# Nine more units of the first token group take seven products in layer two; Sinkhorn's matmuls stand later and in one bank

## The chip, the cores and the metric

The kernel runs on one core of one Trainium2 chip. The metric is device time in microseconds (us): 2010.24 us, the median of three runs (2008.88 to 2013.74). Engines are named as the profile names them: PE is TensorE (PEld its weight loads), DVE VectorE, ACT ScalarE, POOL GpSimd, SP the engine that issues DMAs.

## The reference

Three stages follow each other: windowed attention (4 batches, 8 heads, 576 positions), a two-layer network with a leaky ReLU, and a mixture of eight experts whose token weights come from eight rounds of Sinkhorn scaling. The last stage takes three quarters of the time:

```python
logits = x @ w_gate                       # x: 2304 x 512, 8 experts
P = np.exp(logits - logits.max())
for _ in range(8):
    P /= P.sum(1, keepdims=True) + 1e-09
    P /= P.sum(0, keepdims=True) + 1e-09
    P *= N / E
for e in range(E):
    h = np.maximum(x @ w1[e], 0.0)        # 512 -> 1024
    ye = h @ w2[e]                        # 1024 -> 512
    out += P[:, e:e + 1] * ye
```

## The kernel before

Every fp32 operand is split in two parts, a rounded high part and the rest (the low part), and `three` (L362 to L364) makes three matmuls of one: high by high, high by low, low by high. A split costs one copy on ACT (L1142 for weights) and one subtraction (L585) on DVE or POOL, whichever the planner picks.

The expert stage (function `second`) works through 48 units: three token groups of 768 tokens (`sb_`, 0 to 2), each with 16 half experts (`g`, 0 to 15; a half expert is 512 of the 1024 hidden columns). Unit u is `sb_ = u // 16`, `g = u % 16`. The text calls the token groups the first (units 0 to 15), the second (16 to 31) and the third (32 to 47). In a unit, layer one multiplies two matrices cut in 2x2 blocks by a Strassen-like scheme with seven block products in place of eight (`PRODUCTS`): 84 matmuls of 384 columns into the PSUM tiles W01 and X01. Layer two then works on three token strips, with either the same seven products (three strips of seven products of six matmuls, 126 matmuls of 256 columns; `layer2`) or the plain eight (144 matmuls; `direct`). `plain2(u)` says which; before the change units 2 to 15 are plain and all others take seven.

The two forms load the other engines differently. Seven products need sums of weight blocks (S1 to S4 for layer one, T1 to T4 for layer two) and sums of hidden blocks; each output block is gathered by DVE from six products of 256 columns per strip (L1466). The plain form needs the weights only as they are, and gathers two outputs of 512 columns per strip (L1393). `weights(m, u)` prepares the weights of layer m + 1: it loads the raw block, and then either makes seven operands of it with all their sums ("full": seven ACT copies and eleven block operations on DVE or POOL) and writes what later groups need to DRAM (`wfar`), or makes plain operands alone (four or three copies and as many subtractions), or fetches finished operands from `wfar`. Before the change layer one's weights are made in full in the first group, and layer two's in the second group, because the first group needs them plain. The weights of the first two half experts are made ahead for both layers (`convert_ahead`, eight jobs) during the two-layer network, on ACT and POOL.

Each engine runs its own queue in order. The order is written by a planner: `add` collects operations with an engine (or a choice), a cost, a priority (mostly a due time) and the keys that they read and write; `arrange` walks through simulated time and always starts the ready operation with the lowest priority number. The cost marker "2" tells it that a DVE operation and POOL keep each other out. A PSUM bank, such as SW[1], is a key: whoever writes it waits for the last reader.

Sinkhorn (`sinkhorn`, L1058 to L1097) is a chain: in a round, eight small DVE instructions and one PE matmul (L1087) that sums over partitions into bank SW[1]. Its DVE steps have priority 33, its PE steps -50. Bank SW[1] is also used by layer two of the first units.

Of the kernel before, what the change touches and what calls it, by code (L numbers as in the profile page):

```python
# [13 lines left out]
ALU = mybir.AluOpType  # L14
# [5 lines left out]
DM = H * D  # L20
F1 = 2048
E, F2 = 8, 1024
# [18 lines left out]
HA = SB // 2  # L41
NSB = NT // SB
NG = 2 * E
PRE = 2


def key_start(j):
# [11 lines left out]
def program(tc, qk, v, moe_w_in, moe_w_out, moe_alpha, moe2_w_gate, moe2_w1, moe2_w2, masks, out):  # L59
# [697 lines left out]
    class Op:  # L757


        def __init__(self, engines, emit, prio, deps, slots, seq):  # L760
            self.engines, self.emit, self.prio, self.slots, self.seq = dict(engines), emit, prio, slots, seq
            self.lock = {"POOL"} | ({"DVE"} if len(engines) > 1 and engines[0][0] == "DVE" or "2" in dict(engines) else set())
            self.engines.pop("2", None)
            self.deps, self.next, self.wait, self.ready = deps, [], 0, 0.0

    queue_of, ops = {}, []
    writer, readers = {}, {}
# [27 lines left out]
    def arrange(places, more):  # L795
# [46 lines left out]
        while len(done) < len(ops):  # L842
            best = None
            for e, l in lists.items():
                if l:
                    t = max(now[e], min(at(o, e) for o in l))
                    if best is None or t < best[0]:
                        best = t, e
            assert best is not None, ("stuck", [(b.name, b.left) for c in queue_of for b in queue_of[c][heads[c] : heads[c] + 2]], heads, len(done))
            t, e = best  # L850
            o = min((o for o in lists[e] if at(o, e) <= t), key=lambda o: (o.prio, o.seq))
            cost = o.engines[e]
            for e2 in o.engines:
                lists[e2].remove(o)
            if e in o.lock and e in held:
                held["POOL" if e == "DVE" else "DVE"] = t + cost
            if e == "SP":
                begin = max(t + 1.2, wire[0])
                wire[0] = begin + cost
                end, now[e] = wire[0] + 0.8, t + 0.06  # L860
            else:
                end = now[e] = t + cost
            o.at, o.on, o.end = t, e, end
            done.append(o)
            for c, ats in more.get(o, {}).items():
                free[c] += [(end, at) for at in ats]
                bind(c)
            late = end + (0.25 if e == "PE" else 0.1)
            for x in o.next:
                x.ready = max(x.ready, end if e in x.engines and e != "SP" and len(x.engines) == 1 else late)  # L870
                x.wait -= 1
                if x.wait == 0:
                    enlist(x)
            for b in o.slots:
                b.left -= 1
                b.end = max(b.end, late)
                if b.left == 0:
                    free[b.cls].append((b.end, b.at))
                    bind(b.cls)
        return sorted(done, key=lambda o: o.at)  # L880

    def second():
# [3 lines left out]
        step1, step2 = 29.5 / 7, 29.5 / 21  # L886

        def plain2(u):
            return u < NG and u >= PRE

        begins = [T1ST]
        for u in range(NSB * NG + 2):
# [165 lines left out]
        def sinkhorn():  # L1058
            G = ("SW", 1)
            g = SW[1]  # L1060
            R = "right"
            M = mem

            def v(cost, emit, reads, writes):
                add([("DVE", cost)], emit, 33, [*reads, R], writes)

            V = nc.vector
            v(0.35, lambda _: V.tensor_reduce(M["m1"], lgt.rearrange("p t e -> p (t e)"), axis=AX.X, op=ALU.max), ["lgt"], ["m1"])
            add([("PE", 0.1)], lambda _: nc.tensor.transpose(g[:1, :P], M["m1"], ident), -50, ["m1"], [G])
            v(0.3, lambda _: V.tensor_reduce(M["m2"], g[:1, :P], axis=AX.X, op=ALU.max), [G], ["m2"])  # L1070
            add([("PE", 0.1)], lambda _: nc.tensor.matmul(g[:, 0:1], ones[0:1, :], M["m2"], start=True, stop=True), -50, ["m2"], [G])
            v(0.15, lambda _: V.tensor_scalar(out=M["ng"], in0=g[:, 0:1], scalar1=-1.0, scalar2=None, op0=ALU.mult), [G], ["ng"])
            add([("ACT", 0.4)], lambda _: nc.scalar.activation(M["pt"], lgt, AF.Exp, bias=M["ng"], scale=1.0), -50, ["ng", "lgt"], ["pt"])
            for _ in range(8):
                v(0.29, lambda _: V.tensor_reduce(M["rr"], M["pt"], axis=AX.X, op=ALU.add), ["pt"], ["rr"])
                v(0.38, lambda _: V.tensor_scalar(out=M["rr"], in0=M["rr"], scalar1=EPS, scalar2=None, op0=ALU.add), ["rr"], ["rr"])
                v(0.27, lambda _: V.reciprocal(M["rr"], M["rr"]), ["rr"], ["rr"])
                v(
                    0.31,
                    lambda _: V.tensor_tensor(  # L1080
                        out=M["pt"], in0=M["pt"], in1=M["rr"].unsqueeze(2).to_broadcast([P, NTT, E]), op=ALU.mult
                    ),
                    ["rr", "pt"],
                    ["pt"],
                )
                v(0.44, lambda _: V.tensor_reduce(M["cs"], M["pt"].rearrange("p t e -> p e t"), axis=AX.X, op=ALU.add), ["pt"], ["cs"])
                add([("PE", 0.1)], lambda _: nc.tensor.matmul(g[:, :E], share, M["cs"], start=True, stop=True), -50, ["cs"], [G])  # L1087
                v(0.16, lambda _: V.tensor_scalar(out=M["rc"], in0=g[:, :E], scalar1=EPS * E / NT, scalar2=None, op0=ALU.add), [G], ["rc"])
                v(0.2, lambda _: V.reciprocal(M["rc"], M["rc"]), ["rc"], ["rc"])
                v(  # L1090
                    0.54,
                    lambda _: V.tensor_tensor(
                        out=M["pt"], in0=M["pt"], in1=M["rc"].unsqueeze(1).to_broadcast([P, NTT, E]), op=ALU.mult
                    ),
                    ["rc", "pt"],
                    ["pt"],
                )  # L1097

        def weights(m, u):
# [5 lines left out]
            nd = {n: need(m, u, i) for i, n in enumerate(names)}  # L1105
            cls = ("w1", "w2")[m]
            b = got[m, u] = {}
            full = g >= PRE and sb_ == m
            plain, sums = PLAIN[m], {s[0]: s[1:] for s in SUMS[m]}
            ready = [] if full or eight else [n for n in names if (g, m, n) in wfar]  # L1110
            if full:
# [244 lines left out]
        def direct(u, j, s, t0, tts):  # L1356
# [4 lines left out]
            e = g // 2  # L1361
            scaled = sb_ > 0 or e > 0
            for i, (a, x, r, d) in enumerate(EIGHT):
                ps, K = ((SW[s], ("SW", s)), (SX[s], ("SX", s)))[r - 1]
                t = t0 + 2 * i * step2

                def mm(_, i=i, a=a, x=x, ps=ps, d=d):
# [19 lines left out]

                def out_(_, ps=ps, oi=oi, tt=tt):
                    o, p_ = mem["o"][:, oi], mem["pt"][:, tt, e : e + 1]
                    if not scaled:  # L1390
                        nc.vector.tensor_tensor(out=o, in0=ps, in1=o, op=ALU.add)
                    else:
                        nc.vector.scalar_tensor_tensor(out=o, in0=ps, scalar=p_, in1=o, op0=ALU.mult, op1=ALU.add)  # L1393

                assert g
                add([("DVE", 0.75)], out_, t + 0.7, [K, "right", *okeys] + (["pt"] if scaled else []), okeys)
                if g == NG - 1:
                    send(oi, tt, t)

# [9 lines left out]
        def layer2(u):  # L1409
            sb_, g = divmod(u, NG)  # L1410
            h, w = got["h", u], got[1, u]
            e = g // 2
            scaled = sb_ > 0 or e > 0
            eight = plain2(u)
            for j in range(3):
                k = 3 * u + j
# [7 lines left out]
                for i, (a, x, bk) in enumerate(PRODUCTS):  # L1424
# [30 lines left out]
                    def out_(e_, ps=ps, oi=oi, dh=dh, tt=tt, new=new):  # L1455
                        o = mem["o"][:, oi, dh * FS : (dh + 1) * FS]
                        x = ps[:, :FS]
                        p_ = mem["pt"][:, tt, e : e + 1]
                        if new and not scaled:
                            nc.scalar.copy(o, x)  # L1460
                        elif new:
                            nc.scalar.mul(o, x, p_)
                        elif not scaled:
                            nc.vector.tensor_tensor(out=o, in0=x, in1=o, op=ALU.add)
                        else:
                            nc.vector.scalar_tensor_tensor(out=o, in0=x, scalar=p_, in1=o, op0=ALU.mult, op1=ALU.add)  # L1466

                    rd = [K, "right"] + ([] if new else [ok]) + (["pt"] if scaled else [])
                    add(act(FS, True) if new else dve(FS), out_, t, rd, [ok])
                    if sb_ == 0 and g == 1 and i in (5, 6):  # L1470

                        def scale(_, oi=oi, tt=tt):
                            o = mem["o"][:, oi]
                            nc.scalar.mul(o, o, mem["pt"][:, tt, 0:1])

                        add(act(DM), scale, t, ["pt", ("o", oi, 0), ("o", oi, 1)], [("o", oi, 0), ("o", oi, 1)])
                    if g == NG - 1 and i in (5, 6):
                        send(oi, tt, t)

# [46 lines left out]
    with tc.manual_schedule():  # L1526
# [33 lines left out]
                ahead = 30 if THIRD[0] <= n < THIRD[1] else 6  # L1560
                ready.setdefault(i, []).append((n, which, 12, begin[due] - ahead))
        n_ends = next(i for i, u in enumerate(units) if u[3] == order[-2])
        jobs = [(g, m, st) for g in range(PRE) for m in range(2) for st in range(2)]

        prev = None
        for i, u in enumerate(units[:-1]):
            if i == n_close:
# [5 lines left out]
                prep[0] = pool(sx, "prep", bufs=2, side="right")  # L1573
                pz = pool(sp, "pz", bufs=2, space=PSUM)
                banks += [(pz, "x"), (pz, "y")]
                last = len(units) - 4
                for x, job in enumerate(jobs):
                    pside.add(convert_ahead(*job), 19, begin[i + 3 + (last - i - 3) * (x + 1) // len(jobs)])
            if i >= 2 and units[i - 2][5]:
# [106 lines left out]
```

## Time and profile before

| | us |
|---|---|
| median of three runs | 2010.24 |
| lowest, highest | 2008.88, 2013.74 |
| the profiled execution | 2013.85 |
| its span, first to last instruction | 2012.1 |

The span is the time between the first and the last instruction that the profiler saw; 1.75 us of the profiled execution lie outside it. A matmul's busy time overlaps the next one's, so that PE's pace is read from how many matmuls stand in a stretch in which PE never waits. A unit's first layer-one matmul was taken as its start; units 8 and 14 start at 779.41 and 969.34 us, units 22 and 31 at 1219.24 and 1485.01 us, unit 0 at 522.0 us.

### The profile page before, as it was taken

How to read it: one execution, taken by the hardware profiler on the slowest of the kernel's cores; microseconds unless marked ns; L12 is line 12 of the kernel's file. 1: busy time of each engine (PE TensorE's matmuls, PEld its weight loads, DVE VectorE, ACT ScalarE, POOL GpSimd, SP SyncE). 2: the span in 40 equal slices, each digit the busy share in tenths (PEclk: the TensorE clock that was granted, in tenths of full speed). 3: DMA queues.
4: the chain of work that ended last, by engine and by line, in shares of the span. 5: the costliest groups of instructions: out<-in, count | busy, mean ns of one | idle time of the engine just before them, and what ended most of it. 6: DMA issues, size and time to landing. Idle time of an engine off the chain costs nothing.

```text
span 2012.1 us, 37421 instructions
## 1 busy us (share of the span) xinstructions
PE 1965.2 (98%) x14899; PEld 1940.5 (96%) x14899; DVE 1328.8 (66%) x2142; ACT 894.8 (44%) x1686; POOL 654.6 (33%) x567
## 2 busy tenths in 40 slices
PE   7999999999989999999999999999999999999998
PEld 5889999999979999999999999999999999999998
DVE  6775776764587645454536888778776666766766
ACT  6654444434445434343324545445444434434442
POOL 4434776676343232232200443233330001101100
PEclk8999999999999999999999999999999999999999
DMA  7421333332646845455486786677689667666662
GB/s 234 141 70 53 106 118 98 100 116 81 257 159 256 290 160 207 169 187 195 171 330 222 285 292 230 215 244 244 218 291 343 227 212 233 230 208 224 237 212 84
DMA packets 124014, 399.95 MB, mean 199 GB/s; under 512 B 12736, under 2 KB 41152, under 8 KB 118464
## 3 DMA queue, kind: packets, MB, share of 16 engines
q1 hardware_dynamic: 123840, 397.56, 57.4%
q8 instruction: 117, 1.92, 0.4%
q14 instruction: 57, 0.47, 0.1%
HBM read 283.22 MB, written 114.29 MB: 198 GB/s over the span
## 4 chain that ended last, share of the span: by engine, by line
PE 92%; DVE 4%; POOL 1%; DMA 1%; issue 1%; ACT 1%; SPq 0%; POOLq 0%; DVEq 0%; ACTq 0%
PE SW L364 7%; PE SW L362 7%; PE SW L363 7%; PE W L362 6%; PE W L363 6%; PE W L364 6%; PE SX L364 5%; PE SX L363 5%; PE SX L362 5%; PE X L363 5%; PE X L362 5%; PE X L364 5%; PE psH L362 3%; PE psH L364 3%; PE psH L363 3%; PE psY L362 3%
## 5 line engine op out<-in xcount | busy, mean ns | idle before, releaser
L362 PE MATMUL W<-XS,WT 128*128 128x384 f32 x768 | 260.3, 339 | 1.7 <-DVE WX L1340 1.2
L363 PE MATMUL W<-XS,WT 128*128 128x384 f32 x768 | 259.5, 338 | 0.0
L364 PE MATMUL W<-XS,WT 128*128 128x384 f32 x768 | 259.4, 338 | 0.0
L585 POOL TENSOR_TENSOR WT<-rawR,WT 128x512 fp32r<-128x512 f32 x78 | 104.8, 1345 | 377.4 <-ACT WT L1142 236.2
L362 PE MATMUL X<-XS,WT 128*128 128x384 f32 x576 | 194.4, 338 | 0.0
L1466 DVE SCALAR_TENSOR_TENSOR oR<-SW,pt,oR 128x256 f32<-128x256 f32 x282 | 132.8, 480 | 93.1 <-PE SW L364 91.7
L363 PE MATMUL X<-XS,WT 128*128 128x384 f32 x576 | 193.8, 336 | 0.0
L364 PE MATMUL X<-XS,WT 128*128 128x384 f32 x576 | 193.8, 336 | 0.0
L1466 DVE SCALAR_TENSOR_TENSOR oR<-SX,pt,oR 128x256 f32<-128x256 f32 x270 | 128.0, 479 | 71.6 <-PE SX L364 71.6
L391 POOL TENSOR_TENSOR gl<-u,gh 128x288 fp32r<-128x288 f32 x126 | 107.4, 854 | 154.3 <-ACT gh L390 147.7
L585 POOL TENSOR_TENSOR wR<-rawR,wR 128x512 fp32r<-128x512 f32 x36 | 51.2, 1425 | 314.0 <-ACT wR L1142 233.6
L363 PE MATMUL psH<-XS,WT 128*128 128x288 f32 x504 | 149.7, 297 | 1.3 <-DVE XS L142 1.3
L362 PE MATMUL psH<-XS,WT 128*128 128x288 f32 x504 | 150.7, 299 | 0.1
L364 PE MATMUL psH<-XS,WT 128*128 128x288 f32 x504 | 149.8, 297 | 0.0
L362 PEld LDWEIGHTS W<-XS,WT 128*128 128x128 f32 x768 | 145.6, 190 | 2.2 <-DVE WX L1340 1.4
L363 PEld LDWEIGHTS W<-XS,WT 128*128 128x128 f32 x768 | 145.1, 189 | 0.0
L364 PEld LDWEIGHTS W<-XS,WT 128*128 128x128 f32 x768 | 145.1, 189 | 0.0
L585 POOL TENSOR_TENSOR wR<-RAW,wR 128x512 fp32r<-128x512 f32 x38 | 54.3, 1432 | 252.1 <-ACT wR L1142 124.5
L387 DVE SCALAR_TENSOR_TENSOR u<-neg,rest,psH 128x288 f32<-128x288 f32 x108 | 55.3, 512 | 109.0 <-ACT neg L386 103.6
L363 PE MATMUL psY<-gl,WT 128*128 128x288 f32 x376 | 111.5, 297 | 5.1 <-POOL gl L391 5.0
L362 PE MATMUL psY<-gh,WT 128*128 128x288 f32 x376 | 113.1, 301 | 1.0 <-ACT acc L410 1.0
L364 PE MATMUL psY<-gh,WT 128*128 128x288 f32 x376 | 111.2, 296 | 1.4 <-POOL WT L532 1.4
(268 smaller groups left out, 6577.9 us busy)
## 6 DMA issues: line engine op xcount, KB each, us to landing
RAW<-in_moe_w SPq DMA_DIRECT2D x21, 1024.0 KB, 6.9
rawR<-in_moe_w SPq DMA_DIRECT2D x21, 1024.0 KB, 6.1
WT<-a11g SPq DMA_DIRECT2D x34, 512.0 KB, 4.9
WT<-S2g SPq DMA_DIRECT2D x34, 512.0 KB, 4.5
WT<-a12g SPq DMA_DIRECT2D x34, 512.0 KB, 3.6
WT<-S3g SPq DMA_DIRECT2D x34, 512.0 KB, 3.6
WT<-S1g SPq DMA_DIRECT2D x34, 512.0 KB, 3.7
WT<-a22g SPq DMA_DIRECT2D x34, 512.0 KB, 4.7
```

What stands on the lines that cost most here:

```text
L362: nc.tensor.matmul(ps, lh, rh, start=start, stop=False, skip_group_check=more)
L363: nc.tensor.matmul(ps, lh, rl, start=False, stop=False, skip_group_check=more)
L364: nc.tensor.matmul(ps, ll, rh, start=False, stop=stop, skip_group_check=more)
L387: nc.vector.scalar_tensor_tensor(out=u, in0=neg, scalar=rest[:, ft : ft + 1], in1=ps[:, :CH], op0=ALU.mult, op1=ALU.add)
L391: nc.gpsimd.tensor_tensor(out=gl, in0=u, in1=f(gh), op=ALU.subtract)
L585: eng.tensor_tensor(out=out, in0=x, in1=y, op=op)
L1466: nc.vector.scalar_tensor_tensor(out=o, in0=x, scalar=p_, in1=o, op0=ALU.mult, op1=ALU.add)
```

## The change

`plain2` now follows a list: units 0, 1, 2, 5, 8, 11 and 14 are plain, and the other nine of the first group (3, 4, 6, 7, 9, 10, 12, 13, 15) take seven products. Units 0 and 1, which took seven, become plain. So 7 units are plain in place of 14. `weights` follows: for the nine units both layers' weights are made in full in the first group, and the second group fetches layer two's sums; for the seven plain ones layer two's are still made in full in the second group. Only half expert 0's layer one is made ahead (two jobs in place of eight), and those jobs are due earlier.

Sinkhorn's DVE steps get priority 45 (33 before), its PE steps 45 (-50 before), and a PE step is planned no sooner than 1.5 us after the DVE step that writes its operand (`slack`). Three of its DVE steps per round are marked as keeping POOL out. The plain units 0 and 1 use the banks SW[0], SX[0] and SX[1] in turn, so that only Sinkhorn writes SW[1] until unit 2's layer two. Unit 0's outputs are copied by ACT, unit 1's are added by DVE and then scaled by ACT.

```diff
-PRE = 2
+PRE = 1
+EIGHTH = (0, 1, 2, 5, 8, 11, 14)
...
-                x.ready = max(x.ready, end if e in x.engines and e != "SP" and len(x.engines) == 1 else late)
+                x.ready = max(x.ready, end if e in x.engines and e != "SP" and len(x.engines) == 1 else late + x.slack)
...
         def plain2(u):
-            return u < NG and u >= PRE
+            return u < NG and u in EIGHTH
...
-            def v(cost, emit, reads, writes):
-                add([("DVE", cost)], emit, 33, [*reads, R], writes)
+            def v(cost, emit, reads, writes, both=False):
+                add([("DVE", cost), ("2", 0)][: 1 + both], emit, 45, [*reads, R], writes)
+
+            def pe(emit, reads):
+                add([("PE", 0.1)], emit, 45, reads, [G])
+                ops[-1].slack = 1.5
...
-                add([("PE", 0.1)], lambda _: nc.tensor.matmul(g[:, :E], share, M["cs"], start=True, stop=True), -50, ["cs"], [G])
+                pe(lambda _: nc.tensor.matmul(g[:, :E], share, M["cs"], start=True, stop=True), ["cs"])
...
-            full = g >= PRE and sb_ == m
+            full = (m == 1 or g >= PRE) and sb_ == (m if plain2(g) else 0)
...
-                ps, K = ((SW[s], ("SW", s)), (SX[s], ("SX", s)))[r - 1]
+                ps, K = ((SW[s], ("SW", s)), (SX[s], ("SX", s)))[r - 1] if g > 1 else (
+                    (SW[0], ("SW", 0)),
+                    (SX[0], ("SX", 0)),
+                    (SX[1], ("SX", 1)),
+                )[(2 * j + r - 1) % 3]
...
-                    if not scaled:
+                    if g == 0:
+                        nc.scalar.copy(o, ps)
+                    elif not scaled:
                         nc.vector.tensor_tensor(out=o, in0=ps, in1=o, op=ALU.add)
...
+                if g == 1:
+
+                    def scale(_, oi=oi, tt=tt):
+                        o = mem["o"][:, oi]
+                        nc.scalar.mul(o, o, mem["pt"][:, tt, 0:1])
+
+                    add(act(DM), scale, t + 1, ["pt", *okeys], okeys)
...
-                    add(act(FS, True) if new else dve(FS), out_, t, rd, [ok])
+                    add(act(FS, True) if new else [("DVE", 0.48)], out_, t, rd, [ok])
...
-        jobs = [(g, m, st) for g in range(PRE) for m in range(2) for st in range(2)]
+        jobs = [(g, 0, st) for g in range(PRE) for st in range(2)]
...
-                last = len(units) - 4
+                last = n_ends - 2
```

The first place is the DVE queue at the end of Sinkhorn's first round, in unit 1. Names: rr, pt, cs and rc are Sinkhorn's row sums, weights, column sums and reciprocals; XS, hR and WX hold layer one's results; W_... is the PSUM tile W01. Before:

```order
L1086 TENSOR_REDUCE cs<-pt 128x8
L1088 TENSOR_SCALAR rc<-SW_6935 128x8
L1089 RECIPROCAL rc<-rc 128x8
L1092 TENSOR_TENSOR pt<-pt,rc 128x144
L1075 TENSOR_REDUCE rr<-pt 128x18
L1076 TENSOR_SCALAR rr<-rr 128x18
L1077 RECIPROCAL rr<-rr 128x18
L1080 TENSOR_TENSOR pt<-pt,rr 128x144
```

After:

```order
L1092 TENSOR_REDUCE cs<-pt 128x8
L1286 SCALAR_TENSOR_TENSOR XS<-W_6707,XS 128x768
L1094 TENSOR_SCALAR rc<-SW_6710 128x8
L1095 RECIPROCAL rc<-rc 128x8
L1098 TENSOR_TENSOR pt<-pt,rc 128x144
L1080 TENSOR_REDUCE rr<-pt 128x18
L1081 TENSOR_SCALAR rr<-rr 128x18
L1082 RECIPROCAL rr<-rr 128x18
L586 TENSOR_TENSOR WX<-W_6707,WX 128x768
L586 TENSOR_TENSOR W_6707<-W_6707,WX 128x2x384
L1085 TENSOR_TENSOR pt<-pt,rr 128x144
L1092 TENSOR_REDUCE cs<-pt 128x8
```

Before, a whole round stands together on DVE. Now the drains of layer one (L1286, L586 on W and WX) stand inside a round. On PE, 12 to 24 matmuls stand between two of Sinkhorn's matmuls before, and 42 to 78 now; the eight rounds reach from unit 1 to the middle of unit 3.

The second place is the DVE queue in unit 4, where the next token group's tokens are split as well (the rows of 384 columns). oR is the output, with SW, SX the PSUM banks it is gathered from; RAW and rawR are raw weights, WT and wR split ones. Before:

```order
L1393 SCALAR_TENSOR_TENSOR oR<-SW_6935,pt,oR 128x512
L1393 SCALAR_TENSOR_TENSOR oR<-SX_6936,pt,oR 128x512
L585 TENSOR_TENSOR WT<-RAW,WT 128x512
L585 TENSOR_TENSOR wR<-rawR,wR 128x512 x2
L585 TENSOR_TENSOR WT<-RAW,WT 128x384 x2
L585 TENSOR_TENSOR RAW<-RAW 128x384
L1279 SCALAR_TENSOR_TENSOR hR<-W_6932,hR 128x768
L1393 SCALAR_TENSOR_TENSOR oR<-SW_6934,pt,oR 128x512
L585 TENSOR_TENSOR WT<-RAW,WT 128x384
L1393 SCALAR_TENSOR_TENSOR oR<-SX_6937,pt,oR 128x512
L585 TENSOR_TENSOR WT<-RAW,WT 128x384
L585 TENSOR_TENSOR RAW<-RAW 128x384
```

After:

```order
L1406 SCALAR_TENSOR_TENSOR oR<-SX_6712,pt,oR 128x512
L1481 SCALAR_TENSOR_TENSOR oR<-SW_6709,pt,oR 128x256
L586 TENSOR_TENSOR WT<-rawR,WT 128x384 x2
L586 TENSOR_TENSOR rawR<-rawR 128x384
L586 TENSOR_TENSOR WT<-rawR,WT 128x384
L586 TENSOR_TENSOR rawR<-rawR 128x384
L1481 SCALAR_TENSOR_TENSOR oR<-SX_6712,pt,oR 128x256
L1481 SCALAR_TENSOR_TENSOR oR<-SX_6711,pt,oR 128x256
L586 TENSOR_TENSOR WX<-W_6707,WX 128x768
L586 TENSOR_TENSOR W_6707<-W_6707,WX 128x2x384
L1481 SCALAR_TENSOR_TENSOR oR<-SW_6710,pt,oR 128x256
L1481 SCALAR_TENSOR_TENSOR oR<-SW_6709,pt,oR 128x256
```

The outputs of 512 columns (L1393) are replaced by outputs of 256 columns (L1481), three for one. In unit 4 as a whole (from its first layer-one matmul to unit 5's) DVE has 48 instructions beside 264 matmuls now, 29 beside 228 before; in unit 20 before, the crowded one of the second group, 48 beside 240. In the even part of the first group the three units 9 to 11 now hold 32 subtractions or sums of 512 columns on POOL and 28 on DVE; before, each unit held 7 on POOL and 8 on DVE. In a unit of the third group 2 stand on POOL and 1 on DVE.

## Rows read from the trace of the kernel before

**Rows 1.** The page: its span, TensorE's line, and the granted clock.

```profile
PE 1965.2 (98%) x14899; PEld 1940.5 (96%) x14899; DVE 1328.8 (66%) x2142; ACT 894.8 (44%) x1686; POOL 654.6 (33%) x567
...
PEclk8999999999999999999999999999999999999999
```

**Rows 2.** Windows: busy us and instructions of PE, PEld, DVE, ACT, POOL; clock; DMA.

```profile
779.41:969.34 189.93, 189.93 (x1370) 189.93 (x1369) 91.99 (x120) 75.41 (x114) 54.38 (x43) 1.00 0.53 183
1219.24:1485.01 265.77, 265.77 (x1892) 265.77 (x1891) 210.23 (x316) 128.49 (x199) 90.38 (x64) 1.00 0.69 232
1595.00:1890.00 295.00, 295.00 (x2100) 295.00 (x2099) 203.94 (x320) 121.73 (x180) 27.13 (x20) 1.00 0.68 223
```

**Rows 3.** Waits of TensorE; columns: us in total, times, longest.

```profile
PE SW L1087 <- DVE cs L1086: 8.6, 5, 2.8
...
PE psY L363 <- POOL gl L391: 5.0, 4, 2.8
PE SW L362 <- DVE oR L1466: 4.0, 3, 1.8
...
PE W L362 <- DVE WX L1340: 1.2, 1, 1.2
```

**Rows 4.** Windows at half clock; columns as in rows 2.

```profile
576.10:579.50 3.40, 3.40 (x12) 3.40 (x11) 3.23 (x8) 0.00 (x0) 1.23 (x1) 0.50 0.39 157
589.70:593.10 3.40, 3.40 (x15) 3.40 (x14) 2.35 (x4) 0.53 (x2) 0.00 (x0) 0.50 0.00 0
1193.90:1197.30 3.40, 3.40 (x16) 3.40 (x16) 2.17 (x6) 0.62 (x1) 0.47 (x1) 0.50 1.03 420
```

**Rows 5.** Sinkhorn's matmuls, by tile; columns: ns min/median/max, first and last start.

```profile
L1087 PE MATMUL SW<-cs,share x16: 170/257/278, 555.8 to 588.2; 128*128 128x8 f32 x16
```

**Rows 6.** Tile rr in the same view, on DVE.

```profile
L1076 DVE TENSOR_SCALAR rr<-rr x8: 176/688/1754, 552.8 to 585.2; 128x18 f32<-128x18 f32 x8
```

**Rows 7.** Timeline around the longest wait for POOL; columns: start, us.

```profile
489.48 1.47 POOL L585 TENSOR_TENSOR praw<-praw 128x256 f32<-128x256 f32 x1
...
490.91 0.79 POOL L391 TENSOR_TENSOR gl<-u,gh 128x288 fp32r<-128x288 f32 x1
...
491.75 0.19 PEld L363 LDWEIGHTS psY<-gl,WT 128*128 128x128 f32 x1 [3.08 <-POOL gl L391]
...
491.75 0.40 PE L363 MATMUL psY<-gl,WT 128*128 128x288 f32 x1 [2.84 <-POOL gl L391]
```

**Rows 8.** Groups of instructions, conversions made ahead; busy us, mean ns.

```profile
L585 POOL TENSOR_TENSOR pboth<-praw,pboth 128x256 fp32r<-128x256 f32 x56 | 48.8, 872 | 1.7 <-ACT pboth L640 1.6
```

**Rows 9.** Windows around units 20 and 21; columns as in rows 2.

```profile
1155.08:1185.23 30.15, 30.07 (x215) 29.86 (x214) 27.85 (x44) 17.92 (x31) 16.16 (x13) 1.00 0.73 246
1185.23:1189.63 4.40, 3.55 (x30) 3.34 (x29) 4.37 (x6) 3.67 (x7) 2.31 (x3) 1.00 0.93 343
1189.63:1219.24 29.61, 27.82 (x183) 27.50 (x181) 19.91 (x30) 9.97 (x16) 6.49 (x5) 0.94 0.75 281
```

**Rows 10.** Groups of instructions between 1219.24 and 1485.01 us.

```profile
L585 DVE TENSOR_TENSOR hR<-WX,hR 128x768 fp32r<-128x768 f32 x22 | 26.9, 1251 | 0.0
...
L585 DVE TENSOR_TENSOR XS<-WX,XS 128x768 fp32r<-128x768 f32 x23 | 24.6, 1092 | 0.0
```

**Rows 11.** Line L585 after 600 us; columns as in rows 5.

```profile
L585 DVE TENSOR_TENSOR hR<-WX,hR x85: 944/951/2060, 644.9 to 1993.0; 128x768 fp32r<-128x768 f32 x85
L585 POOL TENSOR_TENSOR WT<-rawR,WT x78: 1282/1297/2026, 635.3 to 1900.3; 128x512 fp32r<-128x512 f32 x78
...
L585 DVE TENSOR_TENSOR wR<-RAW,wR x37: 674/692/694, 687.9 to 1970.8; 128x512 fp32r<-128x512 f32 x37
```

**Rows 12.** Groups of instructions over the whole span; busy us, mean ns.

```profile
L1466 DVE SCALAR_TENSOR_TENSOR oR<-SW,pt,oR 128x256 f32<-128x256 f32 x282 | 132.8, 480 | 93.1 <-PE SW L364 91.7
...
L1142 ACT CAST WT<-rawR 128x512 fp32r<-128x512 f32 x111 | 68.0, 619 | 27.3 <-issue 13.0 <-PE SW L364 5.5 <-DMA rawR<-in_moe_w 5.2
...
L1393 DVE SCALAR_TENSOR_TENSOR oR<-SW,pt,oR 128x512 f32<-128x512 f32 x42 | 31.5, 749 | 6.6 <-PE SW L364 6.5
```

More of the change, by code (lines that the diff above doesn't have):

```diff
@@ L763, in __init__ @@
             self.engines.pop("2", None)
-            self.deps, self.next, self.wait, self.ready = deps, [], 0, 0.0
+            self.deps, self.next, self.wait, self.ready, self.slack = deps, [], 0, 0.0, 0.0
     queue_of, ops = {}, []
@@ L1062, in sinkhorn @@
             M = mem
-            def v(cost, emit, reads, writes):
-                add([("DVE", cost)], emit, 33, [*reads, R], writes)
+            def v(cost, emit, reads, writes, both=False):
[3 more added lines that the diff above has]
+                ops[-1].slack = 1.5
             V = nc.vector
             v(0.35, lambda _: V.tensor_reduce(M["m1"], lgt.rearrange("p t e -> p (t e)"), axis=AX.X, op=ALU.max), ["lgt"], ["m1"])
-            add([("PE", 0.1)], lambda _: nc.tensor.transpose(g[:1, :P], M["m1"], ident), -50, ["m1"], [G])
+            pe(lambda _: nc.tensor.transpose(g[:1, :P], M["m1"], ident), ["m1"])
             v(0.3, lambda _: V.tensor_reduce(M["m2"], g[:1, :P], axis=AX.X, op=ALU.max), [G], ["m2"])
-            add([("PE", 0.1)], lambda _: nc.tensor.matmul(g[:, 0:1], ones[0:1, :], M["m2"], start=True, stop=True), -50, ["m2"], [G])
+            pe(lambda _: nc.tensor.matmul(g[:, 0:1], ones[0:1, :], M["m2"], start=True, stop=True), ["m2"])
             v(0.15, lambda _: V.tensor_scalar(out=M["ng"], in0=g[:, 0:1], scalar1=-1.0, scalar2=None, op0=ALU.mult), [G], ["ng"])
@@ L1075, in sinkhorn @@
                 v(0.29, lambda _: V.tensor_reduce(M["rr"], M["pt"], axis=AX.X, op=ALU.add), ["pt"], ["rr"])
-                v(0.38, lambda _: V.tensor_scalar(out=M["rr"], in0=M["rr"], scalar1=EPS, scalar2=None, op0=ALU.add), ["rr"], ["rr"])
+                v(0.38, lambda _: V.tensor_scalar(out=M["rr"], in0=M["rr"], scalar1=EPS, scalar2=None, op0=ALU.add), ["rr"], ["rr"], True)
                 v(0.27, lambda _: V.reciprocal(M["rr"], M["rr"]), ["rr"], ["rr"])
@@ L1084, in sinkhorn @@
                     ["pt"],
+                    True,
                 )
                 v(0.44, lambda _: V.tensor_reduce(M["cs"], M["pt"].rearrange("p t e -> p e t"), axis=AX.X, op=ALU.add), ["pt"], ["cs"])
[L1087 removed]
+                pe(lambda _: nc.tensor.matmul(g[:, :E], share, M["cs"], start=True, stop=True), ["cs"])
                 v(0.16, lambda _: V.tensor_scalar(out=M["rc"], in0=g[:, :E], scalar1=EPS * E / NT, scalar2=None, op0=ALU.add), [G], ["rc"])
@@ L1096, in sinkhorn @@
                     ["pt"],
+                    True,
                 )
@@ L1393, in out_ @@
                         nc.vector.scalar_tensor_tensor(out=o, in0=ps, scalar=p_, in1=o, op0=ALU.mult, op1=ALU.add)
-                assert g
-                add([("DVE", 0.75)], out_, t + 0.7, [K, "right", *okeys] + (["pt"] if scaled else []), okeys)
+                reads = [K, "right", *(okeys if g else ())] + (["pt"] if scaled else [])
+                add([("DVE", 0.75)] if g else act(DM, True), out_, t + 0.7, reads, okeys)
+                if g == 1:
[3 more added lines that the diff above has]
+                    add(act(DM), scale, t + 1, ["pt", *okeys], okeys)
                 if g == NG - 1:
@@ L1458, in out_ @@
                         p_ = mem["pt"][:, tt, e : e + 1]
-                        if new and not scaled:
-                            nc.scalar.copy(o, x)
-                        elif new:
+                        if new:
                             nc.scalar.mul(o, x, p_)
-                        elif not scaled:
-                            nc.vector.tensor_tensor(out=o, in0=x, in1=o, op=ALU.add)
                         else:
                             nc.vector.scalar_tensor_tensor(out=o, in0=x, scalar=p_, in1=o, op0=ALU.mult, op1=ALU.add)
-                    rd = [K, "right"] + ([] if new else [ok]) + (["pt"] if scaled else [])
-                    add(act(FS, True) if new else dve(FS), out_, t, rd, [ok])
[L1470 to L1476, printed above, removed]
+                    rd = [K, "right", "pt"] + ([] if new else [ok])
+                    add(act(FS, True) if new else [("DVE", 0.48)], out_, t, rd, [ok])
                     if g == NG - 1 and i in (5, 6):
```

1 line of the change is left out of this document (removed).

## The prediction

> **What bounds the kernel now.** I read the page first: PE is busy for 98% of the span and its clock is full in nearly every slice [rows 1]. So the time is PE's work plus what PE waits. PE's pace comes from windows cut at unit starts: in the plain units 8 to 13 and in the seven-product units 22 to 30 PE never idles, and the same holds in the third group [rows 2]. Six plain units take 189.93 us, 31.66 each; nine units of seven products take 265.77 us, 29.53 each. The difference, 2.13 us, is 18 matmuls of 256 columns, 0.118 us each; the 84 of 384 columns take the rest, (31.66 - 144 x 0.118) / 84 = 0.175 us each.
>
> Then the list of PE's waits [rows 3]. Those of the opening (attention) are not touched by the change. Touched are Sinkhorn's matmuls (8.6 us in 5 waits), the two-layer network's wait for a low part from POOL (5.0 us in 4), the first product of unit 1 (1.2 us), and output drains on DVE, of which 1.8 us lie in the crowded unit 20. The clock shows what such waits cost beyond themselves: behind Sinkhorn's waits two windows of 3.4 us run at half clock, which is 1.2 GHz, and behind unit 20's one more [rows 4]; at half clock half of the time is lost, 1.7 us each.
>
> **The change part by part.** The sum starts from the profiled execution, 2013.85 us, which lies 3.6 us above the median of the runs.
>
> *Products.* Seven fewer plain units remove 7 x 18 = 126 matmuls: 7 x 2.13 = 14.9 us, all on PE, the engine that sets the time. Nothing hides this; it can only be given back by new waits.
>
> *Sinkhorn.* Before, a round takes 4.6 us: from 555.8 to 588.2 us there are seven steps between eight matmuls [rows 5]. DVE hands the rounds on back to back, while PE has only 12 to 24 matmuls to put between them; at 0.118 to 0.175 us that is 1.4 to 4.2 us, less than the round. Its DVE steps also stretch: the 18-column add takes 0.18 us at best and 0.69 in the median, 1.75 at worst [rows 6]. Now PE has 42 to 78 matmuls between two of them, 5 to 14 us for the same DVE work. So most of the 8.6 us of waiting goes, with the two half-clock windows behind it (3.4 us) and unit 1's 1.2 us, because unit 0, as a plain unit, no longer makes its sums on DVE at its end: 13.2 us at most, none at least. What is late next is DVE's own queue: drains now stand inside a round, so one or two matmuls may still wait. I leave 2.5 us for that and take 10.7 us.
>
> *Conversions made ahead.* The longest of the network's four waits shows their cause: POOL finishes a step of these conversions, and only then the low part that PE's matmul is waiting for [rows 7]. Eight jobs are 56 splits on POOL, 0.87 us each [rows 8], beside their sums. Two of the eight jobs stay, and they are due before the network's last units. I take a quarter of the waits as staying: 5.0 - 1.25 = 3.75 us gained. The ends are 5.0 (none is left) and 0 (the low parts wait for other POOL work).
>
> *Units 18 to 21.* Unit 20's crowd cost 0.08 + 0.85 + 1.79 = 2.7 us of waits [rows 9] and 1.7 us of half clock, 4.4 us. In its window DVE is busy for 27.85 of 30.15 us. In the second group nine units now fetch layer two's sums and make fewer conversions, but units 16, 17 and 18 still make them in a row, and tokens are still split around units 18 and 20. I keep 1.5 us of the 4.4: 2.9 gained, between 4.4 and 0.
>
> *Units 3 to 7 of the first group.* Here the load becomes what it was in unit 20: 48 DVE instructions stand in unit 4, as in unit 20 before, and the token splits of unit 4 come on top of two sets of weight sums. I price it as a second unit 20: 4.4 us lost. The ends are 0 and 8.8 (it happens in two units).
>
> *The even part of the first group, units 8 to 15.* Nothing in the trace runs two full conversions beside a seven-product unit, so I count DVE's load for two seven-product units and one plain one. A unit of the third group has 203.94 / 295 x 29.53 = 20.4 us of DVE; a plain one 91.99 / 6 = 15.3 [rows 2]. Without their 512-column operations at 0.69 us on DVE [rows 11] (1 and 8 of them), that is 2 x 19.7 + 9.8 = 49.2. The 28 that are there now add 19.3: 68.5 us. DVE and POOL also stretch each other: in units 22 to 30 the two 768-column groups took 26.9 + 24.6 us for 45 instructions [rows 10] whose median is 0.951 [rows 11], 8.7 us more than 45 medians, beside 64 POOL instructions [rows 2], 0.14 us for each. For POOL's 31 or so in three units that is 4.3 us. DVE's 72.8 us stand against PE's 2 x 29.53 + 31.66 = 90.7, 80%; in units 22 to 30 it was 210.23 of 265.77, 79%, without a wait of PE. POOL comes to 31 x 1.41 (90.38 / 64) = 44 us, 48%, against 34% there. ACT copies one operand in 0.62 us [rows 12]: a third-group unit's 121.73 / 10 = 12.2 us and 11 further copies are 19.0, 64% of a unit. So no engine is full, and I expect little: 2 us lost, between 0 and 19 (rival one). DMA moves the writes of layer two's sums for nine half experts from the second group to the first, and adds no wait in my sum: its share there was 0.53, and 0.69 in the second group, which wrote them so far while PE never waited [rows 2]. Per strip the six drains of 0.48 us in place of two of 0.75 [rows 12] are inside these numbers.
>
> *Units 0 and 1.* That ACT copies unit 0's outputs and scales unit 1's, and that their plain outputs rotate over three banks, I price at nothing: ACT has half of the time free [rows 2]. If that cover fails, one more wait like unit 1's 1.2 us comes.
>
> *Sum.* -14.9 - 10.7 - 3.75 - 2.9 + 4.4 + 2 = -25.8 us. From the profiled execution that gives 1988.0; from the median 2010.24, which is what is forecast, 1984.4. I say 1985.
>
> A rule that speaks against the change stands in the Trainium skill, "GPSIMD Engine Reference", section 1 Specifications: POOL's way into SBUF is shared with DVE, and they contend when DVE reads two SBUF operands. The trace agrees in kind: the same 768-column subtraction has a median of 0.951 us and a longest of 2.060 [rows 11]. It is behind rival two.
>
> **The rivals.**
>
> *One: the first group's even part meets waits like unit 20's.* For it: three kinds of units follow each other there, so DVE's load is uneven inside a period. Against it: 80% is what the second group carried without a wait. One wait of 4.4 us in each of the 13 / 3 = 4.3 periods of units 3 to 15 costs 19 us: 1984.4 + 19 = 2003.
>
> *Two, the other side: DVE becomes the bound of the first group.* Each POOL subtraction keeps one DVE instruction out for as long as the worst did, 2.060 - 0.951 = 1.11 us [rows 11]. The 31 in a period add 34 us to 68.5: 102.9 against PE's 90.7, 12 us lost per period, 52 in 4.3 periods: 1984.4 + 52 = 2036, slower than before. It begins to cost when a POOL subtraction takes (90.7 - 68.5) / 31 = 0.72 us from DVE; the second group showed 0.14, five times less.
>
> *Three: Sinkhorn still holds PE up.* Its DVE steps stand behind drains that wait for PE, so each of the eight rounds could stop PE as before, in other units. For it: a DVE instruction that waits holds the whole queue. Against it: at least 5 us of PE's work per round. Then the 10.7 us are not gained: 1995.
>
> **How the numbers follow.** Forecast 69%, rival one 14%, rival three 12%, rival two 5%. The lower end takes every gain at its best: 14.9 + 13.2 + 5.0 + 4.4 = 37.5, 1973, rounded to 1972. The upper end takes in rival three and rival one, 2003. A measurement of this kernel can tell about 0.3%, 6 us, from no change. Faster: forecast, rival three and most of rival one, 0.93. Within 0.3%: the rest of rival one, 0.03. Slower: rival two, 0.04.
>
> **What would show it.** PE has 126 fewer layer-two matmuls, and units 8 to 15 start 29.5 or 31.7 us apart with full PE. Waits of PE for cs fall under 3 us and the two half-clock windows after 576 us are gone. Waits of psY for POOL's low part fall under 2 us. A wait for a DVE drain with a half-clock window appears between units 3 and 7. Units 8 to 15 further apart than 29.5 and 31.7 would mean rival one; DVE over 95% busy in them, rival two; waits for cs over 6 us, rival three. I am wrong if the time is over 2003 or the gain does not come from PE's missing matmuls first.

## The result and the profile after

The changed kernel takes 1976.39 us, the median of four runs (1975.37 to 1978.71); the kernel before, on the same chip, 2010.53. The ratio is 0.983, with a 95% interval of 0.9813 to 0.9847: 34 us gained, 26 forecast. The profiled execution took 1977.1 us, its span 1975.3.

From the page of the changed kernel, the lines that answer to [rows 1]:

```profile
PE 1941.9 (98%) x14773; PEld 1920.0 (97%) x14773; DVE 1400.6 (71%) x2291; ACT 923.7 (47%) x1713; POOL 635.5 (32%) x529
...
PEclk8999999999999999999999999999999999999999
```

The 126 matmuls are gone, POOL has 38 instructions less and DVE 149 more. Where the time went shows when both spans are cut at the same work: behind the network's 450th matmul, then at unit starts.

| stretch | before | after | difference | layer-two matmuls of 256 columns |
|---|---|---|---|---|
| opening | 166.93 | 164.70 | -2.2 | |
| network, to unit 0 | 355.07 | 348.50 | -6.6 | |
| units 0 to 7 | 257.41 | 247.72 | -9.7 | 936, 936 |
| units 8 to 15 | 253.25 | 240.39 | -12.9 | 1152, 1044 |
| units 16 to 21 | 186.58 | 182.37 | -4.2 | 792, 780 |
| units 22 to 30 | 265.77 | 265.65 | -0.1 | 1134, 1128 |
| unit 31 to the end | 527.06 | 526.00 | -1.1 | 2286, 2286 |

The opening's code is unchanged; over the twelve kernels of this case it took 163.7 to 167.0 us, so its 2.2 us are no effect. Units 0 to 7 keep their number of layer-two matmuls: two more plain units stand against two more of seven products that end there.

Three windows of the kernel after, the network, units 8 to 15 and units 22 to 30 (columns as in [rows 2]):

```profile
150.00:512.05 362.05, 362.05 (x2761) 360.02 (x2756) 231.16 (x454) 141.72 (x320) 197.66 (x195) 1.00 0.18 58
760.92:1001.31 240.39, 240.39 (x1718) 240.32 (x1717) 185.74 (x265) 125.74 (x198) 107.68 (x78) 1.00 0.69 258
1183.68:1449.33 265.65, 265.43 (x1887) 264.91 (x1885) 192.69 (x294) 115.99 (x174) 50.12 (x36) 1.00 0.68 227
```

In the first two PE is busy for the whole stretch: no wait for POOL's low parts is left, and the even part of the first group has none although DVE is busy for 77% of it, POOL for 45% and ACT for 52%.

PE's waits in the kernel after (columns as in [rows 3]); the opening's are left out:

```profile
PE SW L363 <- DVE oR L1481: 3.2, 3, 1.7
PE X L363 <- ACT X L1325: 3.0, 2, 2.8
...
PE SX L363 <- ACT SX L1466: 1.4, 3, 0.5
...
PE W L363 <- DMA WT<-a11g: 0.4, 1, 0.4
```

Of [rows 3] the waits for cs (8.6 us), gl (5.0) and WX (1.2) are gone. The second line is new. Sinkhorn's matmuls and the add, by tile (columns as in [rows 5] and [rows 6]):

```profile
L1093 PE MATMUL SW<-cs,share x16: 170/213/256, 554.8 to 619.0; 128*128 128x8 f32 x16
...
L1081 DVE TENSOR_SCALAR rr<-rr x8: 175/794/1053, 550.3 to 611.1; 128x18 f32<-128x18 f32 x8
```

A round now takes 9.2 us (554.8 to 619.0, seven steps) where it took 4.6, and nobody waits for it.

The timeline around the new wait (start, us):

```profile
512.63 0.41 SPq L1142 DMA_DIRECT2D RAW<-in_moe_w  x1
...
513.67 0.43 ACT L999 CAST gh<-u 128x288 fp32r<-128x288 f32 x1 [0.94 <-DVE u L991]
520.03 0.62 ACT L1149 CAST WT<-RAW 128x512 fp32r<-128x512 f32 x1 [5.93 <-DMA RAW<-in_moe_w]
...
521.37 0.80 ACT L1325 COPY X<-W 128x768 f32<-128x768 f32 x1
...
522.22 0.53 PE L363 MATMUL X<-XS,WT 128*128 128x384 f32 x1 [2.75 <-ACT X L1325]
```

ACT stands still for 5.93 us at the first copy of unit 0's layer-two weights, whose load SP issued at 512.63. The bank copy (L1325) that PE needs is behind it in ACT's queue. The kernel before has no weight copy in unit 0, because these operands were made ahead; its first one stands in unit 1:

```profile
558.19 0.62 ACT L1142 CAST WT<-RAW 128x512 fp32r<-128x512 f32 x1 [4.04 <-PE X L363]
```

In the kernel after, a half-clock window follows PE's wait (columns as in [rows 4]):

```profile
522.40:525.80 3.40, 3.40 (x12) 3.40 (x13) 1.78 (x3) 1.16 (x3) 1.18 (x2) 0.51 0.00 0
```

### The profile page after: what moved, and what is told of

Its sections match the earlier page's. It is cut to its first block, busy times and chain, and to the rows that moved or that the text cites. A ratio compares the mean times of both kernels' runs of the same rounds, so it can differ in the third digit from the quotient of the medians.

```text
span 1975.3 us, 37173 instructions
## 1 busy us (share of the span) xinstructions
PE 1941.9 (98%) x14773; PEld 1920.0 (97%) x14773; DVE 1400.6 (71%) x2291; ACT 923.7 (47%) x1713; POOL 635.5 (32%) x529
## 4 chain that ended last, share of the span: by engine, by line
PE 94%; DVE 2%; DMA 2%; ACT 1%; POOL 0%; issue 0%; SPq 0%; DVEq 0%; ACTq 0%; POOLq 0%
PE W L363 7%; PE W L364 7%; PE W L365 7%; PE SW L365 7%; PE SW L363 7%; PE SW L364 7%; PE SX L365 5%; PE SX L363 5%; PE SX L364 5%; PE X L363 5%; PE X L364 5%; PE X L365 5%; PE psY L363 3%; PE psH L363 3%; PE psH L365 3%; PE psH L364 3%
## 5 line engine op out<-in xcount | busy, mean ns | idle before, releaser
L1481 DVE SCALAR_TENSOR_TENSOR oR<-SW,pt,oR 128x256 f32<-128x256 f32 x363 | 170.1, 479 | 139.1 <-PE SW L365 133.5
L1481 DVE SCALAR_TENSOR_TENSOR oR<-SX,pt,oR 128x256 f32<-128x256 f32 x351 | 167.0, 479 | 91.5 <-PE SX L365 91.0
L586 POOL TENSOR_TENSOR WT<-rawR,WT 128x512 fp32r<-128x512 f32 (+1 forms) x73 | 95.4, 1313 | 313.5 <-ACT WT L1149 164.9
L586 POOL TENSOR_TENSOR WT<-RAW,WT 128x512 fp32r<-128x512 f32 x61 | 84.5, 1390 | 211.4 <-ACT WT L1149 147.1
L586 POOL TENSOR_TENSOR wR<-RAW,wR 128x512 fp32r<-128x512 f32 x41 | 57.6, 1407 | 244.6 <-ACT wR L1149 162.9
L1271 ACT CAST hR<-WX 128x768 fp32r<-128x768 f32 x127 | 104.3, 834 | 67.0 <-DVE WX L1347 64.0
L586 DVE TENSOR_TENSOR hR<-WX,hR 128x768 fp32r<-128x768 f32 x127 | 125.5, 1004 | 1.4 <-ACT hR L1271 1.1
L586 POOL TENSOR_TENSOR wR<-rawR,wR 128x512 fp32r<-128x512 f32 x32 | 45.6, 1428 | 228.4 <-ACT wR L1149 86.4
```

The source lines that it names most:

```text
L586: eng.tensor_tensor(out=out, in0=x, in1=y, op=op)
L1271: add(act(n2), lambda _: nc.scalar.copy(hv(h[n])[:, 0], tm[i]), prio, [("t", i)], [(h[n], "h")])
```

## The experiments

The theory, A in most of the expectations: PE sets the time, so the terms of the sum are separate pieces of PE's line and each part of the change gives its own piece. Against it stands in each case a B in which the piece comes from elsewhere or is limited by another engine; each expectation names its own.

**All sixteen units plain** (`e1_all_plain`): Sinkhorn and the conversions as after, no seven-product unit in the first group.

```diff
-EIGHTH = (0, 1, 2, 5, 8, 11, 14)
+EIGHTH = tuple(range(16))
```

> Edit: the changed kernel with all 16 units of the first group plain; everything else (Sinkhorn's place and bank, one half expert converted ahead) stays. Theory A (the nine units' gain is PE's matmuls alone: 9 x 2.13 = 19.2 us, less the 2.0 us of waits between units 3 and 7 that go again): 1976.4 + 19.2 - 2.0 = 1993.6 us, and no PE wait over 0.3 us between units 3 and 16. Theory B (the nine units also lose or win elsewhere, such as a changed second group): at least 3 us away from that, under 1990.6 or over 1996.6.

Measured 1993.64 us, ratio to before 0.9913 (0.9898 to 0.9928), so 17.3 us over the change. Units 8 to 15, by windows:

```profile
764.74:1017.86 253.12, 253.12 (x1826) 253.12 (x1825) 120.38 (x157) 97.11 (x146) 67.46 (x53) 1.00 0.57 204
```

PE is full here as it was after the change, with DVE busy for 120 us in place of 186: the 65 us more that the change puts on DVE cost PE nothing there. Outside the opening the two profiled executions are 14.9 us apart: the nine units' 9 x 2.13 = 19.2 us, less 2.8 us of waits that the change has more in units 3 to 7 and 16 to 22, and 1.5 us that are not placed and may stand around these waits. A holds. That the median meets its 1993.6 to the tenth is luck: 2.3 of the 17.3 us between the two profiled executions are the opening's.

**Sinkhorn at its old place, its own bank kept** (`e2_old_place`):

```diff
-                add([("DVE", cost), ("2", 0)][: 1 + both], emit, 45, [*reads, R], writes)
+                add([("DVE", cost)], emit, 33, [*reads, R], writes)
...
-                add([("PE", 0.1)], emit, 45, reads, [G])
-                ops[-1].slack = 1.5
+                add([("PE", 0.1)], emit, -50, reads, [G])
```

> Edit: the changed kernel with Sinkhorn's old priorities (DVE 33, PE -50), without the 1.5 us and without the marks that keep POOL out; the bank of its own and the plain units 0 and 1 stay. Theory A (the place in PE's queue removed the waits): waits of PE for cs come back, about 8 us with 3.4 us of half clock behind them, 1976.4 + 8 to 12 = 1984 to 1988 us. Theory B (the bank of its own, or the plain units 0 and 1, removed them): no wait for cs over 2 us in all, 1975 to 1978 us.

Measured 1983.64 us, 0.9865 (0.9851 to 0.988). The waits for cs are back, and the matmuls stand between 547.8 and 579.9 us:

```profile
PE SW L1092 <- DVE cs L1091: 3.7, 7, 1.1
```

```profile
L1092 PE MATMUL SW<-cs,share x16: 170/256/277, 547.8 to 579.9; 128*128 128x8 f32 x16
```

The profiled span is 6.3 us longer than after, 5.6 of it in units 0 to 7. The place is a cause, as A says, but less than A forecast: it brings back only 3.7 of the 8.6 us of [rows 3], none of them over 1.1 and none with a half-clock window. So the other half of Sinkhorn's gain does not hang on the place: it came with the own bank or with the plain units 0 and 1, which this run keeps both. The traces show how: at the old priorities 18 to 30 matmuls stand between two of Sinkhorn's here, where 12 to 24 did in the kernel before. The marks that keep POOL out were taken away with the priorities and not by themselves.

**The bank shared, the late place kept** (`e3_shared_bank`):

```diff
-                ps, K = ((SW[s], ("SW", s)), (SX[s], ("SX", s)))[r - 1] if g > 1 else (
-                    (SW[0], ("SW", 0)),
-                    (SX[0], ("SX", 0)),
-                    (SX[1], ("SX", 1)),
-                )[(2 * j + r - 1) % 3]
+                ps, K = ((SW[s], ("SW", s)), (SX[s], ("SX", s)))[r - 1]
```

> Edit: the changed kernel with units 0 and 1 using the same four banks in layer two as the other units, so that they share SW[1] with Sinkhorn, whose late place stays. Theory A (the bank is needed for the late place): unit 0's third strip has to wait in the plan until Sinkhorn has ended, so PE's reserve of matmuls between two of Sinkhorn's is smaller or PE waits for banks; 1980 to 1990 us. Theory B (the place alone does it): 1975 to 1978 us.

Measured 1982.38 us, 0.9863 (0.9846 to 0.9879). No wait for cs, but another one:

```profile
PE SW L363 <- DVE oR L1477: 4.6, 2, 2.9
```

The 2.9 us stand at 671.5 us, 68 us after Sinkhorn's last matmul (603.5 us), with a half-clock window behind them. The time is A's, its cause is not. PE's reserve did fall, to 30 to 66 matmuls between two of Sinkhorn's, but no wait came of that; the wait came out in unit 4, where the change itself has its waits, and that the shared bank put it there through the planner's order is not shown. Only 3.4 us of the loss lie in units 0 to 7; 1.5 are the opening's and 1.3 follow a half-clock window at the program's end. What the bank is worth by itself stays open.

**All eight conversion jobs made ahead again** (`e4_ahead_back`; at their old due times, and six of the results are not read):

```diff
...
-        jobs = [(g, 0, st) for g in range(PRE) for st in range(2)]
+        jobs = [(g, m, st) for g in range(2) for m in range(2) for st in range(2)]
...
-                last = n_ends - 2
+                last = len(units) - 4
```

> Edit: the changed kernel with all eight jobs of conversions ahead as before; the outcome of the six additional jobs goes to DRAM and is read by nothing. Theory A (POOL's steps of these jobs made the two-layer network's matmuls wait for low parts): waits of psY for POOL come back, 4 to 6.5 us in all, 1980.4 to 1983 us. Theory B (other things in that stretch made them wait): under 1.5 us of such waits, 1976 to 1978 us.

Measured 1985.36 us, 0.9878 (0.9864 to 0.9893): 9.0 us over the change. The waits of psY and the 56 splits:

```profile
PE psY L364 <- POOL gl L392: 4.3, 4, 2.8
```

```profile
L586 POOL TENSOR_TENSOR pboth<-praw,pboth 128x256 fp32r<-128x256 f32 x56 | 49.6, 886 | 1.7 <-ACT pboth L641 1.6
```

The network takes 355.52 us against 348.50 in every kernel with two jobs: 7.0 us, of which 4.3 are waits and 1.7 a half-clock window. This is the cause, and it is larger than expected. The other 2 us between the medians are not the network's.

**Unit 0's weight copies later in ACT's queue** (`e5_late_copies`):

```diff
                 add(act(512), lambda _: nc.scalar.copy(wide(b[n])[:, 0], blk(i)), p_, [(r, i)], [(b[n], "h")])
+                ops[-1].slack = 4.0 * (u == 0)
```

> Edit: the changed kernel with the ACT copies of unit 0's layer-two weights planned no sooner than 4 us after their load is planned to land. Theory A (the new wait of 2.75 us in unit 0, with half clock behind it, comes from ACT's queue standing at a copy whose load has not landed, with PE's bank copy X behind it): the wait of X for ACT goes, and 1976.4 - 2.75 - 1.7 = 1972 us. Theory B (the bank copy would be late anyway): the wait stays over 2 us, 1975 to 1978 us.

Measured 1973.63 us, 0.9816 (0.9802 to 0.9831). The timeline of ACT:

```profile
517.16 0.78 ACT L1326 COPY X<-W 128x768 f32<-128x768 f32 x1 [0.57 <-PE W L365]
...
519.01 2.18 ACT L1149 CAST WT<-RAW 128x512 fp32r<-128x512 f32 x4 [0.72 <-DMA RAW<-in_moe_w]
```

The bank copy now stands ahead of the weight copies, PE's wait of 2.75 us and its half-clock window are gone, and units 0 to 7 are 4.0 us shorter. So the new wait was the queue's order, not the load itself. A's 1972 us are missed by 1.6, as much as the end of the profiled execution takes longer with a half-clock window that the change did not have there.

**The nine units alone in the kernel before** (`e6_only_nine`):

```diff
+EIGHTH = (2, 5, 8, 11, 14)
...
-            return u < NG and u >= PRE
+            return u < NG and u in EIGHTH
...
-            full = g >= PRE and sb_ == m
+            full = g >= PRE and sb_ == (m if plain2(g) else 0)
```

> Edit: the kernel before with the nine units on seven products alone (units 0 and 1 as before, both half experts converted ahead, Sinkhorn in its old place). Theory A (the parts add up): 2010 - 19.2 + 2.0 of waits between units 3 and 7 - 3 of unit 20's crowd = 1990 us, Sinkhorn's 8 us of waits stay. Theory B (the nine units need the late Sinkhorn or the plain first units, because the first units' DVE is then too full): waits between units 2 and 7 of 8 us or more, over 1996 us.

Measured 1993.43 us, 0.9919 (0.9904 to 0.9933): 17 us gained, 20 expected. Its waits:

```profile
PE SW L1088 <- DVE cs L1087: 8.6, 5, 2.8
...
PE SW L363 <- DVE oR L1467: 4.9, 5, 1.9
PE psY L364 <- POOL gl L392: 4.2, 4, 2.8
```

Sinkhorn's waits stay to the tenth and the network's nearly, and unit 4 gets 1.9 us with a half-clock window behind. Half of the change's gain is the products; the other half needs the other edits. The parts add up, within 3.4 us of A's 1990.

**Five, and three, plain units** (`e7_five_plain`, `e8_three_plain`), to find where DVE's load begins to cost:

```diff
-EIGHTH = (0, 1, 2, 5, 8, 11, 14)
+EIGHTH = (0, 1, 2, 6, 11)
```

```diff
-EIGHTH = (0, 1, 2, 5, 8, 11, 14)
+EIGHTH = (0, 1, 2)
```

> Edit: the changed kernel with two further units on seven products (plain: 0, 1, 2, 6, 11). Theory A (PE bound as long as DVE is under some 85%): 1976.4 - 2 x 2.13 = 1972 us, no wait over 0.5 us between units 8 and 16. Theory B (80% was the edge): waits there of 4 us or more, 1976 us or more.

> Edit: the changed kernel with all units from 3 on on seven products. By the count of the prediction, a unit of two full conversions has 19.7 us on DVE without them and 22 operations of 512 columns; with half of them on POOL DVE has 19.7 + 7.6 + 1.5 = 28.8 of 29.5 us. Theory A (DVE becomes the bound): waits of PE for DVE spread over units 4 to 15, more than the 4 x 2.13 = 8.5 us gained; 1976 to 2000 us. Theory B (the planner moves enough to POOL): 1968 to 1972 us.

Measured 1987.06 us, 0.9886 (0.987 to 0.9902), and 2006.44, 0.9979 (0.997 to 0.9988). Each has fewer matmuls than the change, 36 and 72, and each is slower: the first as its B says, the second as its A says, but beyond that range's 2000 us. Units 8 to 15 of the first, by windows:

```profile
761.30:1009.00 247.70, 243.18 (x1719) 242.22 (x1718) 201.20 (x286) 135.94 (x217) 136.12 (x99) 0.99 0.69 256
```

And of the second, with its waits and the timeline before the longest:

```profile
764.60:1027.20 262.60, 244.78 (x1688) 240.48 (x1686) 225.59 (x313) 141.99 (x229) 151.87 (x106) 0.99 0.70 256
```

```profile
PE SW L363 <- DVE oR L1481: 14.3, 9, 4.0
PE SX L363 <- DVE oR L1481: 7.4, 7, 1.9
...
PE W L363 <- DVE WX L1347: 4.3, 3, 3.0
```

```profile
964.76 1.77 DVE L586 TENSOR_TENSOR RAW<-RAW 128x512 f32<-128x512 f32 x1
966.46 1.75 DVE L586 TENSOR_TENSOR WT<-RAW,WT 128x512 fp32r<-128x512 f32 x1
...
965.94 1.72 POOL L586 TENSOR_TENSOR wR<-rawR,wR 128x512 fp32r<-128x512 f32 x1
967.62 1.72 POOL L586 TENSOR_TENSOR WT<-RAW,WT 128x512 fp32r<-128x512 f32 x1
...
969.00 0.47 DVE L1481 SCALAR_TENSOR_TENSOR oR<-SW,pt,oR 128x256 f32<-128x256 f32 x1
...
969.52 0.58 PE L363 MATMUL SW<-WT,XS 128*128 128x256 f32 x1 [3.95 <-DVE oR L1481]
```

Two splits of 0.69 us on DVE [rows 11] take 1.77 and 1.75 beside two of POOL's, which take 1.72 in place of 1.30; the drain that PE waits for stands behind them, and PE stops for 3.95 us. The longest wait of `e7_five_plain` there, 3.22 us at 982.73, has the same two splits in front of it, at 1.78 and 1.75 us. With DVE at 77% (the change) units 8 to 15 have no wait; at 81% they have four, 4.5 us; at 86% twelve of over 0.4 us, 17.5 us in all. No engine that helps PE is full on average in any of them. POOL's share rises with DVE's, from 45% over 55% to 58%, and the runs do not part the two. This is rival two's mechanism, two steps further than the change goes. The rule that the prediction weighed (the Trainium skill, "GPSIMD Engine Reference", section 1 Specifications: POOL shares its way into SBUF with DVE) agrees with these rows.

**The other plain units one place earlier, with the late copies** (`e9_shift_plain`):

```diff
-EIGHTH = (0, 1, 2, 5, 8, 11, 14)
+EIGHTH = (0, 1, 2, 4, 7, 10, 13)
...
+                ops[-1].slack = 4.0 * (u == 0)
```

> Edit: the kernel with the late copies, and the same number of plain units, but shifted by one: 0, 1, 2, 4, 7, 10, 13, so that unit 4, in which the tokens are split, is plain. Theory A (the 2.0 us of waits in unit 4 come from the six narrow drains per strip and the token splits on DVE together): they go, and 1973.6 - 2 = 1971.6 us. Theory B (what crowds DVE there is the ramp into two full conversions): waits of about 2 us stay, in unit 3, 5 or 6, 1973 to 1976 us.

Measured 1969.54 us, 0.979 (0.9776 to 0.9803), the best of all. Page and waits:

```profile
PE 1940.8 (99%) x14773; PEld 1920.2 (98%) x14773; DVE 1400.6 (71%) x2295; ACT 923.1 (47%) x1713; POOL 628.9 (32%) x525
```

```profile
PE SW L363 <- DVE oR L1482: 2.4, 2, 1.7
...
PE W L363 <- DMA WT<-a11g: 1.2, 1, 1.2
```

With unit 4 plain, the unit in which tokens are split has less to do (40 DVE instructions, busy for 24.7 us, in place of 48 and 31.1), and of the waits of units 3 to 7 only 0.70 us is left; the 1.7 us of the first line are the program's end, as before. One wait for a load, 1.2 us, came up in the second group. Units 0 to 7 are 2.0 us shorter than in `e5_late_copies`, as A says; the end, without that run's half-clock window, gives 1.6 more.

**No slack ahead of Sinkhorn's matmuls** (`e10_no_slack`, with the late copies):

```diff
-                ops[-1].slack = 1.5
```

> Edit: the kernel with the late copies, without the 1.5 us that each of Sinkhorn's PE steps is planned behind its operand; priorities, marks and bank stay, and 24 to 78 matmuls stand between two of Sinkhorn's. Theory A (the distance in PE's queue that the later priorities make is enough): waits for cs under 0.5 us, 1973 to 1974.5 us. Theory B (the 1.5 us do it): waits for cs of 1 to 4 us in all, 1975 to 1978 us.

Measured 1972.1 us, 0.9798 (0.9785 to 0.9811), not to be told from `e5_late_copies`. Its matmuls still stand 24 to 78 others apart, and none waits:

```profile
L1092 PE MATMUL SW<-cs,share x16: 170/214/257, 551.7 to 603.0; 128*128 128x8 f32 x16
```

The distance that the priorities make does it; the slack is worth nothing that can be measured.

## Why the prediction was right, and which terms were off

The mechanism and the direction were right, and the time lies in the range. From 2013.85 the sum went to 1988.0; the profiled execution took 1977.1, 10.9 us less, of which 2.2 are the opening's.

- *Products*, -14.9: right. 126 matmuls less, 108 of them in units 8 to 15, where 12.86 us / 108 = 0.119 us each; forecast 0.118.
- *Sinkhorn*, -10.7: mis-sized. I left 2.5 us for remaining waits; none remained. With unit 1's wait and two half-clock windows 13.2 us are gone, the end of my range. The mechanism, more matmuls for PE while DVE works on a round, fits the traces: 12 to 24 between two of Sinkhorn's with 8.6 us of waits, 18 to 30 with 3.7 (`e2_old_place`), 30 to 66 (`e3_shared_bank`) and 42 to 78 with none. I did not say which part of the change makes this reserve: the old place cost 5.6 us in units 0 to 7, and whether the rest is the bank's or the plain units' is open. Unit 1's wait of 1.2 us stands in `e6_only_nine` and neither in `e2_old_place` nor in `e3_shared_bank`, so it went with the plain units 0 and 1, as forecast.
- *Conversions ahead*, -3.75: mis-sized, 6.6 to 7.0 measured, beyond my end of 5.0. I kept a quarter of the waits for two jobs that cost nothing, and priced a wait at its length alone. The network holds the same 2627 matmuls in both traces; outside its gaps (5.1 us, none after) it still lost 1.4, so 0.36 for each of four waits; in `e4_ahead_back` and `e6_only_nine`, with 1.7 us taken off for half clock, 0.25 each. [rows 7] shows a part of that: the first matmul behind a wait takes 0.40 us, 0.30 in the median elsewhere.
- *Units 18 to 21*, -2.9: about right. Gaps of 2.7 us and 1.7 of half clock before, 1.0 and none after: -3.4. The stretch of units 16 to 21, less its twelve matmuls' 1.4 us, gives -2.8.
- *Units 3 to 7*, +4.4: mis-sized. The wait came in unit 4 as forecast, three times (0.49 us for a copy on ACT, 0.27 and 1.22 for a drain on DVE), but without a half-clock window: 2.0 us. In `e9_shift_plain`, where unit 4 is less crowded, unit 4 has none.
- *Even part*, +2: none. Units 8 to 15 start 29.5 to 29.6 or 31.6 us apart, with DVE at 77% for 80% forecast, POOL at 45% for 48%; ACT at 52%, where the forecast's 64% was for a seven-product unit alone. DVE's block operations there (L586) stretched as priced: 71 of 512 columns took 0.844 us in the mean, 0.691 in the median, and 50 of 768 columns 0.996 and 0.951; that is 10.9 + 2.3 us beside 77 of POOL's, 0.17 us for each, forecast 0.14.
- *Units 0 and 1*, at nothing: the step that failed. I named ACT's free half as the cover and looked at the outputs' copies and scales only. But what is no longer made ahead must be made in the units: unit 0's layer-two weights are now copied by ACT there, and I had counted that only as a gain in the network. A queue in order that stands at a load has no free time, however low its share. It cost 2.75 us and 1.7 of half clock, where I had 1.2 as the price of a failed cover; `e5_late_copies` gives 4.0 back.

So four terms were too cautious and one was missed, in the other direction; that they cancel in part is luck. As measured the terms make -31.7 us, and the stretches outside the opening -34.5. The 2.9 us between are not placed: units 0 to 7 lost 9.7 us where the terms give 6.8, and three small waits that went there (0.16, 0.49 and 0.45 us) are 1.1 of that. Rival one (19 us in the even part) and rival three (waits for cs) did not come; rival two's mechanism is real, as `e8_three_plain` shows, but begins beyond the change. Where it begins was wrong in the prediction, which compared averages: at 0.72 us of DVE for each POOL subtraction. Counted as above, units 8 to 15 of `e7_five_plain` have 0.19 and those of `e8_three_plain` 0.30, and PE already waits.

## What to carry to other kernels

Here a mean share of 77% on a helper engine cost nothing and 81% already did: what counts is whether a drain stands behind two long instructions just when TensorE needs the bank, so move loads away from the crowded unit before removing them. An engine's free time is no cover when its queue holds a copy of data that a DMA has not yet landed ahead of the instruction that matters; look for what stands in front. Price a wait of TensorE at its length and some 0.25 to 0.36 us more, with half clock as a possible extra. Work that is no longer done ahead has to be priced where it goes.

## What the runs showed that was not expected

The length of a wait does not tell whether half clock follows. The network's wait of 2.84 us had no such window before (491.75 us), but the same wait had one in `e4_ahead_back` and `e6_only_nine`; one of 3.04 us in `e8_three_plain` (799.81) had none, and unit 20's 1.79 us had one [rows 4]. At the program's end the same wait of 1.73 us had none in the change and one in `e5_late_copies`, where the last stretch took 527.6 us against 526.0. With the opening's spread that is up to 5 us between two traces of the same code, which is why the stretches above are compared rather than the spans.
